# Reading ranks and list sums on ScalarE ahead of the turning back, in an attention and MoE kernel on one core

## The chip, the core and the metric

The kernel runs on one core of a Trainium2 chip. TensorE (PE), VectorE (DVE), ScalarE (ACT) and GpSimd (POOL) run their own instruction streams in program order and meet at semaphores. SyncE (SP) issues most of the DMAs. The metric is device time of one launch in microseconds; the runs of the kernel before took 1053.6, 1046.92 and 1043.89 us, so the median is 1046.92 us. The profiled execution took 1044.68 us and its span from the first to the last instruction is 1042.8 us.

## The reference

Attention with rotated queries and keys over 8 batches of 8 heads, 576 positions and 64 dimensions; then a mixture of experts over the 4608 tokens, where each token goes to the one expert with the largest logit.

```python
q_rot, k_rot = rotate(q), rotate(k)
scores = scale * q_rot @ k_rot.transpose(0, 1, 3, 2)
attn = exp(scores - max); attn /= sum + 1e-09
x = (attn @ v).transpose(0, 2, 1, 3).reshape(B * S, H * D)      # 4608 x 512
logits = x @ w_gate;  e_idx = argmax(logits, axis=1)
gate_w = softmax(logits)[e_idx];  eom = sigmoid(x @ w_output_gate)
for e in range(8):                                              # 512 -> 1024 -> 512
    out[mask_e] = gate_w * eom[:, e] * (relu(x[mask_e] @ w1[e]) @ w2[e])
```

All values are float32. The kernel splits each float32 factor of the scores and of the expert products into a high and a low part and adds three products.

## The kernel before, in words

**Two stages.** The first 540 us or so are the attention, the rest the experts. The attention goes over 32 pairs of heads, four pairs to a batch. A pair has nine steps, one for each unit of 128 rows of scores (the fifth unit holds the last 64 rows of both heads). A unit's scores are six matmuls into a PSUM tile `sc` (`score`, L493), of which there are two. DVE takes their maximum (`peak`, L498), ACT the exponential (`exp`, L507), DVE turns the result by 32x32 blocks (`turn`, L513), and PE multiplies it with the values (`values`, L535). Units go two by two, except the fifth, which goes alone; the program order of one group is: scores, maxima and exponentials of its units, and then, unit by unit, the work that has been put at that step.

**The accumulator of a pair.** The products with the values of a pair go to one PSUM tile `acc` of four banks, of which there is one. Two pairs after its scores, at the second step of a pair, five matmuls turn it back to rows by token and multiply it with the gates (`back`, L553), from a copy in SBUF that ACT made (`evict`, L542 to L544). DVE then divides by the sums (`divide`, four instructions from L560) into `xb`, the rows of the batch. The next pair's products with the values wait until that is done, since they write the same tile. In the traces here, the starts of L560 mark the pace of the attention: one per pair.

**Sorting tokens to experts.** While the next batch's attention runs, the tokens of the batch before are placed (`place`). Its pieces `s0` to `s21` are put at steps counted from PLACE after the batch's last pair; the table `fs` holds (step, place within the step, piece). Three pieces matter here. At step 17 `s14` multiplies the one-hot choices into unused columns of bank 2 of `acc` (the tile that is turned back in that same step): the ranks of the tokens within their expert. `s14b` has DVE add them to the offsets `base` (L690) and to the counts `cnt` (L691). Five times `ones` (L714, DVE) and `places` (L721, POOL) make 0/1 rows from the ranks; `s20` multiplies them into bank 1 of a later pair's `acc` (L729), and `s21` has DVE add the result to `lists` (L732). Both DVE additions stand behind `back` and ahead of `divide` in program order.

**POOL** rotates and splits the keys and queries of coming pairs (L437, L441, L419) and does the small sums of `place`. **SP** loads keys and queries (`raw`, L425), values (`v`, L432) and later the weights, and stores `xb` to the table `xd` in three pieces (`store`, L668, L670). Batch 6 is an exception (`ahead`): its last steps fall behind the end of the attention, and POOL fetches the first tokens of the experts (L1025) beside its first ones.

Of the kernel before, what the change touches and what calls it, by code (L numbers as in the profile page):

```python
# [15 lines left out]
ALU = mybir.AluOpType  # L16
# [6 lines left out]
E, FF = 8, 1024  # L23
P = 128
# [3 lines left out]
NCH = 5  # L28
# [29 lines left out]
PIECES = ((0, 4), (4, 8), (8, 13), (13, 18))  # L58
PLACE, PM = 20, 3
LISTED = 44  # L60
ROWS, PLACES = (28, 30, 32, 37, 39), (25, 29, 31, 34, 38)

TURN = 1

# [178 lines left out]
class Attention:  # L243


    def __init__(self, tc, nb, pools, cc, ident, ii, first, trib, oneb, cnt, zero, qk, v, xd, row, lists):
# [34 lines left out]
        for n, pr in enumerate(self.pairs):  # L281
            g, b = 9 * n, n // NP
            fs = {"kh": lambda pr=pr: pr.keyhi("A"), "kl": lambda pr=pr: pr.keylo("P"),
                  "qh": lambda pr=pr: pr.queryhi("A"), "ql": lambda pr=pr: pr.querylo("P"), "lasts": pr.lasts, "den0": pr.den0, "den1": pr.den1, "den2": pr.den2, "evict": pr.evict, "back": pr.back,
                  "newxb": lambda pr=pr, b=b: newxb(b) if pr.hp == 0 else None}
            fs["divide"] = lambda pr=pr, b=b: pr.divide(xbs[b])
            for t in range(2):
                fs[f"mult{t}"] = lambda pr=pr, t=t: pr.mult("P", t)
                fs[f"add{t}"] = lambda pr=pr, t=t: pr.add("P", t)
                fs[f"load{t}"] = lambda pr=pr, t=t: pr.load(t)  # L290
                fs[f"loadv{t}"] = lambda pr=pr, t=t: pr.loadv(t)
            for k, (b0, b1) in enumerate(PIECES):
                fs[f"av{k}"] = lambda pr=pr, b0=b0, b1=b1: [pr.values(j) for j in range(b0, b1)]
            early = dict(PREP.get(n, ()))
            for name, o, k in EVENTS:
                if n > 1 or name not in ("load1", "load0", "mult1", "add1", "kh", "kl", "mult0", "add0", "qh", "ql")[:10 if n == 0 else 2]:
                    at(g + early.get(name, o), k, fs[name])
            if n % NP == NP - 1:
                fs = place(tc, (px, px2, small), self.pairs, b, NT, cc, trib, oneb, cnt, xbs, xd, row, lists)
                if b == nb - 1:  # L300
                    self.last = fs
                else:
                    for k, p, f in fs:
                        at(g + PLACE + k, p, f)
# [57 lines left out]
class Pair:  # L362
# [183 lines left out]
    def back(self):  # L546

        parts = []
        for c in range(NCH):
            o = PO if c < 4 else PO + BW  # L550
            parts.append((self.acc[:, c % 4, o:o + BW], self.ac[:, c, :, :].rearrange("p a x -> p (a x)")))
        for out, x in parts:
            self.nc.tensor.matmul(out, x, self.ii[:, self.hp, :], start=True, stop=True, skip_group_check=True)  # L553
# [25 lines left out]
def place(tc, pools, pairs, b, NT, cc, trib, oneb, cnt, xbs, xd, row, lists):  # L579

    nc = tc.nc
    p1, p2, small = pools

    last, ahead = b == NT // S - 1, b == NT // S - 2
    V = nc.vector if last else nc.gpsimd
    tt = V.tensor_tensor
    b3 = lambda t: t.unsqueeze(2).broadcast_to((P, NCH, E))
    T = {}

    def new(n, sh, dt=F32, **k):  # L590
        T[n] = p2.tile(sh, dt, tag=n, name=f"{n}{b}", **k)
        return T[n]
# [56 lines left out]
    def add(c):  # L649
        tt(out=T["ohs"][:, c + 1, :], in0=T["ohs"][:, c, :], in1=T["ohb"][:, c, :], op=ALU.add)  # L650

    def s10():
        V.tensor_scalar(T["eg"], T["eg"], 1.0, None, op0=ALU.add)

    def s11():
        tt(out=T["eg"], in0=T["eg"], in1=T["sm"], op=ALU.mult)

    def s12():
        nc.vector.reciprocal(T["eg"], T["eg"])

    def s13():

        V.tensor_copy(xbs[b][:, :, DM], T["eg"])

    def store(i):
        r, n = b * S + i * 2 * P, 2 if i < 2 else 1
        if i < 2:
            nc.sync.dma_start(out=xd[r:r + 2 * P, :].rearrange("(c p) d -> p c d", p=P), in_=xbs[b][:, 2 * i:2 * i + 2, 0:XW])  # L668
        else:
            nc.sync.dma_start(out=xd[r:r + QR, :], in_=xbs[b][0:QR, 4, 0:XW])  # L670
# [10 lines left out]
    def s14():  # L681
# [3 lines left out]
        nc.tensor.matmul(flat(rk), oneb, flat(T["ohs"]), start=True, stop=False, skip_group_check=True)  # L685
        nc.tensor.matmul(flat(rk[:, 0:NCH, :]), trib, flat(T["ohb"]), start=False, stop=True, skip_group_check=True)

    def s14b():
        tt, rk = nc.vector.tensor_tensor, T["rk"]
        tt(out=new("pr", CE), in0=rk[:, 0:NCH, :], in1=T["base"].unsqueeze(1).broadcast_to((P, NCH, E)), op=ALU.add)  # L690
        tt(out=cnt, in0=rk[:, NCH, :], in1=cnt, op=ALU.add)  # L691

# [3 lines left out]
    def s16():  # L696
        nc.vector.tensor_reduce(new("po", [P, NCH]), T["pr"], axis=AX.X, op=ALU.add)
# [11 lines left out]
    def ones(c):  # L709

        if c == 0:
            new("ro", [P, NCH, lists.shape[1]], F32R, bufs=1)
            new("no", [P, NCH])
        nc.vector.tensor_scalar(T["ro"][:, c, :], row, T["hr"][:, c:c + 1], 0.0, op0=ALU.is_equal, op1=ALU.add,  # L714
                                accum_out=T["no"][:, c:c + 1])

    def places(c):

        if c == 0:
            new("pl", [P, NCH, P], F32R, bufs=1)  # L720
        V.tensor_scalar(T["pl"][:, c, :], row[:, 0:P], T["lo"][:, c:c + 1], T["tok"][:, c:c + 1], op0=ALU.is_equal,  # L721
                                op1=ALU.mult)
# [6 lines left out]
            nc.tensor.matmul(T["ls"], T["pl"][0:m, c, :], T["ro"][0:m, c, :], start=(c == 0), stop=(c == 4), skip_group_check=True)  # L729

    def s21():
        nc.vector.tensor_tensor(out=lists, in0=T["ls"], in1=lists, op=ALU.add)  # L732

    def both(f, c):
        return lambda: (f(), add(c))
# [1 line left out]
    no = lambda: None  # L737
    stores = lambda: [store(i) for i in range(3)]
    if last:
        run = lambda *fs: lambda: [f() for f in fs]  # L740
        return [s0, run(s1, s2), s3, run(s4, s5), run(s6, s7), run(s8, add0), both(s9, 1), lambda: [add(c) for c in (2, 3, 4)],
                run(s10, s11, s12), run(s13, base), no, no, no, no, s14, no, s14b, run(s15, s16, s17)] + [
                lambda c=c: (ones(c), places(c)) for c in range(NCH)] + [stores, no, s20, no, s21, no]

    def adds(*cs):
        return lambda: [add(c) for c in cs]

    fs = [(0, 2, s0), (2, 2, s1), (3, 2, s2), (5, 2, s3), (8, 2, s4), (9, 2, s5), (10, 2, s6), (11, 2, s7), (12, 2, add0),
          (12, 2, adds(1, 2)), (13, 2, adds(3, 4)), (15, 2, s8), (15, 2, base), (17, 1, s14), (17, 2, s14b), (18, 2, s9),
          (19, 2, lambda: (s10(), s11())), (20, 2, s15), (22, 2, lambda: (s16(), s12())), (23, 2, s17)]  # L750
    listed = LISTED - 9 if ahead else LISTED
    fs += [(listed, 1, s20), (listed, 2, s21)]
    fs += [(26 + c if ahead else ROWS[c], 3, lambda c=c: ones(c)) for c in range(NCH)]
    fs += [(26 + c if ahead else PLACES[c], 3, lambda c=c: places(c)) for c in range(NCH)]

    if b == NT // S - 2:
        fs += [(37, 2, lambda: (s13(), stores()))]
    else:
        fs += [(25, 2, s13), (31, 2, lambda: store(0)), (33, 2, lambda: store(1)), (34, 2, lambda: store(2)), (37, 2, no)]
    return fs  # L760


# [493 lines left out]
```

## Time and profile before

| | |
|---|---|
| median of 3 runs | 1046.92 us (1043.89 to 1053.6) |
| the profiled execution | 1044.68 us, span 1042.8 us, mean granted TensorE clock 0.990 |
| busy share of the span | PE 93%, DVE 78%, ACT 59%, POOL 57% |
| chain that ended last | PE 60%, DVE 13%, POOL 10%, issue 8%, ACT 6% |

The page lists the busy time of every engine, the chain of waits that ended last, and the groups of instructions. A timeline row has the start, the time from the first start to the last end, the engine and line, the instruction with its output and inputs, how many stand in the row, and in brackets the engine's idle time before it with what ended it. "issue" is idle time that ends without a wait which the profile shows.

### The profile page before, as it was taken

To read this page: it belongs to the slowest core of one execution; us is meant where nothing else is said; L and a number is where in the kernel's file an instruction comes from. 1 tells how busy PE (TensorE), PEld (TensorE's weight loads), DVE (VectorE), ACT (ScalarE), POOL (GpSimd) and SP (SyncE) were. 2 spreads that over 40 slices of the span, in tenths; PEclk is the share of its full clock that TensorE was granted. 3 is DMA by queue.
4 is the path that set the end of the run, shared out by engine and by line. 5 is a ranking of instruction groups with operands and counts; after the bars stand their busy time and mean duration, and the time that the engine had idled before them with its cause. 6 is when DMAs were issued, how large, how long until landed. Compare 5 with 4: busy or idle time off the path is not lost.

```text
span 1042.8 us, 34822 instructions
## 1 busy us (share of the span) xinstructions
PE 969.2 (93%) x14461; PEld 844.4 (81%) x14461; DVE 818.0 (78%) x1371; ACT 616.8 (59%) x1283; POOL 599.6 (57%) x613
## 2 busy tenths in 40 slices
PE   4999999989999999999799999999999999999995
PEld 4778777767878777777678899998889988899984
DVE  6889989979988898998768777667776867857772
ACT  4656656656655566665445455557766765857762
POOL 4777898887988879889640122206343443443621
PEclk9999999999999999999999999999999999999998
DMA  6665664666745657465548966767886977977860
GB/s 218 164 173 130 179 195 128 177 163 167 198 125 163 185 159 205 118 179 147 160 140 299 300 211 201 230 201 254 312 299 216 356 243 268 325 283 257 299 240 29
DMA packets 58209, 216.32 MB, mean 207 GB/s; under 512 B 9351, under 2 KB 9660, under 8 KB 53952
## 3 DMA queue, kind: packets, MB, share of 16 engines
q1 hardware_dynamic: 50304, 194.03, 59.9%
q0 software_dynamic: 6464, 18.92, 5.0%
q8 instruction: 115, 1.88, 0.8%
q10 hardware_dynamic: 1280, 1.11, 0.3%
q14 instruction: 46, 0.38, 0.1%
HBM read 196.04 MB, written 20.09 MB: 207 GB/s over the span
## 4 chain that ended last, share of the span: by engine, by line
PE 60%; DVE 13%; POOL 10%; issue 8%; ACT 6%; DMA 1%; ACTq 0%; POOLq 0%; DVEq 0%
PE py L1132 17%; PE ph L1090 14%; PE sc L493 11%; PE acc L535 9%; DVE m L498 5%; POOL raw L437 4%; PE ph L1082 4%; ACT pm L507 4%; DVE pt L513 2%; DVE wl L1049 2%; PE acc L553 2%; POOL raw L441 1%; PE mtp L1055 1%; POOL q L419 1%; ACT wh L1047 1%
## 5 line engine op out<-in xcount | busy, mean ns | idle before, releaser
L507 ACT ACTIVATE pm<-sc,m 128x576 f32<-128x576 f32 x288 | 211.1, 737 | 208.7 <-DVE m L498 207.5
L1049 DVE TENSOR_TENSOR wl<-wr,wh 128x1024 fp32r<-128x1024 f32 x184 | 251.9, 1381 | 45.2 <-ACT wh L1047 42.8
L498 DVE TENSOR_REDUCE m<-sc 128x1 f32<-128x576 f32 x288 | 205.7, 748 | 58.6 <-PE sc L493 57.6
L535 PE MATMUL acc<-pt,v 32*64 32x128 f32 (+1 forms) x9216 | 201.3, 298 | 31.2 <-issue 18.5
L493 PE MATMUL sc<-kh,q 64*128 64x288 f32 x1024 | 205.2, 325 | 20.7 <-ACT q L411 9.7
L1132 PE MATMUL py<-wh,ht 128*128 128x512 f32 x640 | 215.4, 401 | 0.0
L1047 ACT CAST wh<-wr 128x1024 fp32r<-128x1024 f32 x208 | 212.6, 1050 | 0.0
L513 DVE STREAM_TRANSPOSE pt<-pm 128x576 f32<-128x576 f32 x288 | 208.9, 753 | 0.0
L535 PEld LDWEIGHTS acc<-pt,v 32*64 32x64 f32 x9216 | 160.9, 133 | 57.1 <-issue 38.9
L493 PEld LDWEIGHTS sc<-kh,q 64*128 64x128 f32 x1024 | 153.1, 191 | 53.6 <-ACT pm L507 23.1
L437 POOL TENSOR_TENSOR raw<-raw,rt 128x1152 f32<-128x1152 f32 x62 | 163.9, 2643 | 0.3
L1090 PE MATMUL ph<-xt,wh 128*128 128x256 f32 x896 | 161.1, 282 | 0.5 <-DVE xt L1071 0.5
L1132 PEld LDWEIGHTS py<-wh,ht 128*128 128x128 f32 x640 | 120.3, 188 | 25.7
L1090 PEld LDWEIGHTS ph<-xt,wh 128*128 128x128 f32 x896 | 138.3, 188 | 2.4 <-DVE xt L1071 1.2
L493 PE MATMUL sc<-kl,q 64*128 64x288 f32 x512 | 129.7, 308 | 0.0
L1090 PE MATMUL ph<-xt,wl 128*128 128x256 f32 x448 | 126.1, 281 | 0.0
L1132 PE MATMUL py<-wl,ht 128*128 128x512 f32 x320 | 125.9, 393 | 0.0
L1049 POOL TENSOR_TENSOR wl<-wr,wh 128x1024 fp32r<-128x1024 f32 x24 | 58.3, 2431 | 90.4 <-ACT wh L1047 84.4
L441 POOL TENSOR_TENSOR raw<-raw 128x576 f32<-128x576 f32 x62 | 87.6, 1413 | 1.9
L1106 ACT ACTIVATE ht<-ph 128x512 fp32r<-128x512 f32 x56 | 33.4, 597 | 90.3 <-PE ph L1090 90.3
L493 PEld LDWEIGHTS sc<-kl,q 64*128 64x128 f32 x512 | 86.3, 192 | 0.2 <-DVE kl L419 0.2
L1090 PEld LDWEIGHTS ph<-xt,wl 128*128 128x128 f32 x448 | 84.3, 188 | 0.1
(247 smaller groups left out, 1317.4 us busy)
## 6 DMA issues: line engine op xcount, KB each, us to landing
wr<-in_w SPq DMA_DIRECT2D x208, 512.0 KB
raw<-in_qk SPq DMA_DIRECT2D x64, 576.0 KB
v<-in_v SPq DMA_DIRECT2D x128, 288.0 KB
xd<-xb SPq DMA_DIRECT2D x16, 513.0 KB
xd<-xb SPq DMA_DIRECT2D x8, 128.2 KB
rt<-in_rope ACTq DMA_DIRECT2D x1, 576.0 KB
xg<-xd,2idx POOLq DMA_INDIRECT x18, 6.7
out<-y,2idx POOLq DMA_INDIRECT x18, 3.9
```

The lines of the kernel that those rows point to most:

```text
L437: self.eng(eng).tensor_tensor(out=rv, in0=rv, in1=self.rt[:, 2 * t:2 * t + 2, x], op=ALU.mult)
L441: self.eng(eng).tensor_tensor(out=r[:, 2 * t, x], in0=r[:, 2 * t, x], in1=r[:, 2 * t + 1, x], op=ALU.add)
L493: self.nc.tensor.matmul(self.ps[i][:, a, :HS], st, mov[r, x], start=(n == 0), stop=(n == 2))
L498: nc.vector.tensor_reduce(self.m[i], ps[:, :, :HS], axis=AX.XY, op=ALU.max, negate=True)
L507: nc.scalar.activation(pe.rearrange("p (a b) -> p a b", a=2), self.ps[i][:, :, :HS], AF.Exp, bias=self.m[i], scale=1.0, accum_out=self.z[: ...
L513: self.nc.vector.transpose(out=self.pt[:, st[0] + 5 * st[1] if st else 4, :], in_=self.pc.pop(i))
L535: nc.tensor.matmul(self.acc[h * D:h * D + D, a, o:o + 32 * n], self.v[r, h, j, :], self.pt[r, u:u + n, 32 * j:32 * j + 32], start=(j == 0) ...
L1047: self.nc.scalar.copy(wh, r)
L1049: eng.tensor_tensor(out=wl, in0=r, in1=wh.bitcast(F32), op=ALU.subtract)
L1082: nc.tensor.matmul(ph[:, 0, :], st[:, dc, 0:P], mv[:, dc, :], start=(n == 0), stop=(n == 11))
L1090: nc.tensor.matmul(ph[:, f, :], st[:, dc, fs], mv[:, dc, :], start=(n == 0), stop=(n == 11))
L1132: self.nc.tensor.matmul(py[h], st[:, f, hs], mv, start=(f == 0 and n == 0), stop=(f == 7 and n == 2))
```

## The change

Ranks: ACT copies the ranks from PSUM to a new tile `rc` as soon as `s14` has made them (`s14c`, put ahead of `back` in the same step), and POOL makes the two additions of `s14b` from that copy one step later. Lists: ACT copies the sums to `lc`, put ahead of `back`, and POOL adds them to `lists` one step later (`s22`). `back` writes the banks in the order 0, 3, 0, 1, 2. `base` moves from step 15 to step 6. `ones` moves from steps 28, 30, 32, 37, 39 to 29, 29, 38, 38, 42 (for batch 6 from 26 to 30 to 29, 29, 29, 33, 33). The second and third store move from steps 33 and 34 to 40 and 42.

```diff
-ROWS, PLACES = (28, 30, 32, 37, 39), (25, 29, 31, 34, 38)
+ROWS, AHEAD, PLACES = (29, 29, 38, 38, 42), (29, 29, 29, 33, 33), (25, 29, 31, 34, 38)
...
     def back(self):
         parts = []
-        for c in range(NCH):
+        for c in (0, 3, 4, 1, 2):
...
+    def s14c():
+        rc = new("rc", [P, NCH + 1, E])
+        nc.scalar.copy(rc, T["rk"])
+        T["rk"] = rc
+
     def s14b():
-        tt, rk = nc.vector.tensor_tensor, T["rk"]
+        rk = T["rk"]
         tt(out=new("pr", CE), in0=rk[:, 0:NCH, :], in1=T["base"].unsqueeze(1).broadcast_to((P, NCH, E)), op=ALU.add)
         tt(out=cnt, in0=rk[:, NCH, :], in1=cnt, op=ALU.add)
...
     def s21():
-        nc.vector.tensor_tensor(out=lists, in0=T["ls"], in1=lists, op=ALU.add)
+        if last:
+            nc.vector.tensor_tensor(out=lists, in0=T["ls"], in1=lists, op=ALU.add)
+            return
+        nc.scalar.copy(new("lc", [P, lists.shape[1]], bufs=1), T["ls"])
+
+    def s22():
+        nc.gpsimd.tensor_tensor(out=lists, in0=T["lc"], in1=lists, op=ALU.add)
...
-          (12, 2, adds(1, 2)), (13, 2, adds(3, 4)), (15, 2, s8), (15, 2, base), (17, 1, s14), (17, 2, s14b), (18, 2, s9),
+          (12, 2, adds(1, 2)), (13, 2, adds(3, 4)), (6, 2, base), (15, 2, s8), (17, 1, s14), (17, 1, s14c), (18, 2, s14b), (18, 2, s9),
...
-    fs += [(listed, 1, s20), (listed, 2, s21)]
-    fs += [(26 + c if ahead else ROWS[c], 3, lambda c=c: ones(c)) for c in range(NCH)]
+    fs += [(listed, 1, s20), (listed, 1, s21), (listed + 1, 2, s22)]
+    fs += [((AHEAD if ahead else ROWS)[c], 3, lambda c=c: ones(c)) for c in range(NCH)]
...
-        fs += [(25, 2, s13), (31, 2, lambda: store(0)), (33, 2, lambda: store(1)), (34, 2, lambda: store(2)), (37, 2, no)]
+        fs += [(25, 2, s13), (31, 2, lambda: store(0)), (40, 2, lambda: store(1)), (42, 2, lambda: store(2)), (37, 2, no)]
```

TensorE's stream at the ranks of the first batch (step 17), before; L685 and L686 are `s14`, L553 is `back`, L493 the scores of the next two units, and a name in brackets is the engine whose semaphore the instruction waits for:

```order
L493 MATMUL sc_1_2076<-kh_1826,q_1915 128x288
L685 LDWEIGHTS oneb [waits Activation_49]
L685 MATMUL acc_1834<-ohs_1948,oneb 128x48 [waits Pool_49]
L686 LDWEIGHTS trib
L686 MATMUL acc_1834<-ohb_1918,trib 128x40
L553 MATMUL acc_1834<-ii,ac_117 128x160 x5
L493 MATMUL sc_2_2119<-kh_1826,q_1915 128x288 [waits Activation_49]
```

The same place in the changed program:

```order
L493 MATMUL sc_1_2076<-kh_1828,q_1917 128x288
L685 LDWEIGHTS oneb [waits Activation_49]
L685 MATMUL acc_1836<-ohs_1950,oneb 128x48 [waits Pool_49]
L686 LDWEIGHTS trib
L686 MATMUL acc_1836<-ohb_1920,trib 128x40
L553 MATMUL acc_1836<-ii,ac_117 128x160 [waits Activation_49]
L553 MATMUL acc_1836<-ii,ac_117 128x160 x4
L493 MATMUL sc_2_2118<-kh_1828,q_1917 128x288 [waits PE_49]
```

The first matmul of `back` has got a wait for ACT, and the scores behind it have lost theirs.

ScalarE's stream at that place in the changed program; L507 are the exponentials of the two units of this step, L690 is the copy of `s14c`, L465 belongs to the next pair:

```order
L543 COPY ac_117<-acc_1836 64x64
L544 COPY ac_117<-acc_1836 64x64
L507 ACTIVATE pm_0_2093,z_115<-sc_0_2075,m_0_2089 128x576 [waits DVE_49,Activation_49,Pool_49]
L507 ACTIVATE pm_1_2095,z_115<-sc_1_2076,m_1_2091 128x576 [waits DVE_49,Activation_49]
L690 COPY rc_2102<-acc_1836 128x48 [waits PE_49]
L465 CAST bd_114<-q_1917 64x2x64 [waits Pool_49]
```

The copy stands behind both exponentials; before, L465 followed them directly. The copy of the list sums stands at the same place, three pairs further on.

VectorE's stream in the pair with the first `ones`, before (L714):

```order
L498 TENSOR_REDUCE m_4_2502<-sc_4_2495 128x1 [waits DVE_49,PE_49]
L513 STREAM_TRANSPOSE pt_2386<-pm_3_2449 128x576 [waits Activation_49]
L498 TENSOR_REDUCE m_5_2557<-sc_5_2543 128x1 [waits DVE_49,PE_49]
L498 TENSOR_REDUCE m_6_2559<-sc_6_2544 128x1 [waits DVE_49,PE_49]
L513 STREAM_TRANSPOSE pt_2386<-pm_4_2504 128x576 [waits Activation_49]
L714 TENSOR_SCALAR ro_2492,no_2493<-row,hr_2330 128x288
L513 STREAM_TRANSPOSE pt_2386<-pm_5_2561 128x576 [waits Activation_49]
```

and in the changed program (L719):

```order
L498 TENSOR_REDUCE m_4_2501<-sc_4_2494 128x1 [waits DVE_49,PE_49]
L513 STREAM_TRANSPOSE pt_2388<-pm_3_2451 128x576 [waits Activation_49]
L719 TENSOR_SCALAR ro_2541,no_2542<-row,hr_2332 128x288 x2
L498 TENSOR_REDUCE m_5_2560<-sc_5_2546 128x1 [waits DVE_49,PE_49]
L498 TENSOR_REDUCE m_6_2562<-sc_6_2547 128x1 [waits DVE_49,PE_49]
L513 STREAM_TRANSPOSE pt_2388<-pm_4_2503 128x576 [waits Activation_49]
```

Two of them now stand together ahead of the maximum of the sixth unit, and none stands between two transposes.

## Rows read from the trace of the kernel before

**Rows 1.** Busy time by stretch: length, busy us of each engine, PE clock, DMA.

```profile
110.00:460.00 350.00, 320.78 (x7669) 269.64 (x7668) 308.66 (x598) 208.73 (x570) 297.44 (x343) 0.99 0.59 163
600.00:900.00 300.00, 299.13 (x1954) 270.09 (x1953) 215.45 (x293) 186.85 (x264) 106.15 (x69) 1.00 0.75 255
```

**Rows 2.** Timeline of DVE: starts of the division, L560, one per pair.

```profile
109.87 0.68 DVE L560 TENSOR_TENSOR xb<-acc,rz 128x512 f32<-128x512 f32 x1
125.75 0.68 DVE L560 TENSOR_TENSOR xb<-acc,rz 128x512 f32<-128x512 f32 x1
140.77 0.65 DVE L560 TENSOR_TENSOR xb<-acc,rz 128x512 f32<-128x512 f32 x1
157.99 0.65 DVE L560 TENSOR_TENSOR xb<-acc,rz 128x512 f32<-128x512 f32 x1
174.31 0.68 DVE L560 TENSOR_TENSOR xb<-acc,rz 128x512 f32<-128x512 f32 x1
...
271.89 0.65 DVE L560 TENSOR_TENSOR xb<-acc,rz 128x512 f32<-128x512 f32 x1
287.63 0.65 DVE L560 TENSOR_TENSOR xb<-acc,rz 128x512 f32<-128x512 f32 x1
```

**Rows 3.** Timeline of DVE at the ranks of the first batch.

```profile
122.19 1.42 DVE L498 TENSOR_REDUCE m<-sc 128x1 f32<-128x576 f32 x2 [0.19 <-PE sc L493]
...
125.56 0.20 DVE L690 TENSOR_TENSOR pr<-acc,base 128x40 f32<-128x40 f32 x1 [0.61 <-POOL base L673]
```

**Rows 4.** Timeline of PE at the ranks of the first batch.

```profile
122.64 0.18 PE L686 MATMUL acc<-ohb,trib 128*128 128x40 bf16 x1
122.67 1.60 PE L553 MATMUL acc<-ii,ac 128*128 128x160 f32 x10
...
127.02 1.35 PE L535 MATMUL acc<-pt,v 32*64 32x160 f32 x64 [1.28 <-issue]
```

**Rows 5.** Timeline of ACT at the ranks of the first batch.

```profile
122.15 0.21 ACT L544 COPY ac<-acc 64x64 f32<-64x64 f32 x1
...
123.80 0.73 ACT L507 ACTIVATE pm<-sc,m 128x576 f32<-128x576 f32 x1
...
124.51 0.60 ACT L465 CAST bd<-q 64x128 fp32r<-64x128 f32 x2
```

**Rows 6.** Timelines of DVE, PE and ACT at the list of the first batch.

```profile
170.61 1.42 DVE L498 TENSOR_REDUCE m<-sc 128x1 f32<-128x576 f32 x2 [0.27 <-PE sc L493]
...
173.74 0.46 DVE L732 TENSOR_TENSOR lists<-acc,lists 128x288 f32<-128x288 f32 x1 [0.36 <-PE acc L553]
...
172.07 1.62 PE L553 MATMUL acc<-ii,ac 128*128 128x160 f32 x10
...
170.01 0.58 ACT L542 COPY ac<-acc 128x512 f32<-128x512 f32 x1
...
172.91 0.59 ACT L465 CAST bd<-q 64x128 fp32r<-64x128 f32 x2
```

**Rows 7.** Timeline of DVE: a wait for scores, and one of `ones`.

```profile
116.08 1.42 DVE L498 TENSOR_REDUCE m<-sc 128x1 f32<-128x576 f32 x2 [0.86 <-PE sc L493]
...
149.53 0.47 DVE L714 TENSOR_SCALAR_CACHE_REDUCE ro<-row,hr 128x288 fp32r<-128x288 bf16 x1
```

**Rows 8.** Timeline of PE: a stop without a wait, and a gap followed by slower matmuls.

```profile
216.03 0.41 PE L493 MATMUL sc<-kh,q 64*128 64x288 f32 x2 [2.05 <-issue]
...
321.84 1.97 PE L535 MATMUL acc<-pt,v 32*64 32x160 f32 x64 [1.27 <-issue]
```

**Rows 9.** Busy time by stretch, with the PE clock, behind two gaps.

```profile
217.00:220.00 3.00, 3.00 (x84) 2.68 (x82) 2.60 (x6) 1.55 (x4) 3.00 (x2) 0.50 0.70 207
516.00:524.00 8.00, 4.06 (x75) 3.46 (x76) 4.13 (x11) 1.65 (x5) 3.04 (x7) 0.57 1.00 362
```

**Rows 10.** Timeline of DVE at the ranks of batch 6.

```profile
511.26 1.42 DVE L498 TENSOR_REDUCE m<-sc 128x1 f32<-128x576 f32 x2 [0.19 <-PE sc L493]
...
518.49 0.20 DVE L690 TENSOR_TENSOR pr<-acc,base 128x40 f32<-128x40 f32 x1 [4.46 <-POOL base L673]
```

**Rows 11.** Timeline of PE at the list of batch 6.

```profile
548.12 1.62 PE L553 MATMUL acc<-ii,ac 128*128 128x160 f32 x10
```

## The prediction, made before the run

> **What bounds the kernel now.** I read the stretches first. In the attention no engine is full: over 350 us PE is busy for 320.8 us and DVE for 308.7 [rows 1], so the pace is set by who waits for whom within a pair. In the expert stage PE is busy for 299.1 of 300 us [rows 1]; what the attention loses or gains before it moves the end by as much. Next I read the starts of the division, one per pair [rows 2]. From 125.75 to 140.77 is a pair with almost no sorting work: 15.02 us. The pair with the ranks before it took 15.88, the one with three `ones` after it 17.22, the one with two `ones` and the list 16.32. In a quieter batch the pair with three `ones` took 15.74 (271.89 to 287.63). What the change can touch is this excess over 15.0 us.
>
> **The ranks, batches 0 to 5.** Before, the maxima of the two units start at 122.19 and the division at 125.75, behind DVE's wait of 0.61 us for POOL's `base` and the two additions [rows 2, 3]. `back` was not in the way: PE started it at 122.67, right behind `s14`, and took 1.60 us [rows 4]. The change takes wait and additions off DVE. But the order of the changed program shows a wait for ACT on the first matmul of `back`, none on the other four, and none for ACT any more on the scores that follow, which had waited for the exponentials before. So the first one waits for something behind both exponentials, and what stands there is the copy to `rc`. ACT reaches it at 124.51 [rows 5]. 48 columns cost at most the 0.21 us of a copy with 64 [rows 5]; with 0.1 us for the signal `back` starts at 124.82, ends 1.60 later at 126.42, and the division starts at about 126.5: 0.75 us later than before, six times: **+4.5**. DVE's saved work doesn't count, since DVE waits anyway. POOL's two extra sums lie in its waits for ACT.
>
> Which banks must wait is also a matter of rule. The Trainium skill, PSUM — Partial Sum Buffer, section "PSUM bank collisions raise a hardware error", says that two engines must not be in the same bank and quadrant at once and that different banks run clean; by that `back` could begin in banks 0 and 3 while ACT reads bank 2. No row of before shows the two together. In the sum I follow the wait in the program; the other case is the first rival.
>
> **The lists, batches 0 to 5.** Before, DVE waited 0.36 us for `back`, added for 0.46 and divided at 174.31 [rows 2, 6]. Now `back` waits for the copy to `lc`, which ACT reaches at 172.91 instead of the L465 there [rows 6]. 288 columns lie between 0.21 us for 64 [rows 5] and 0.58 for 512 [rows 6]; on the line between them 0.40. `back` then starts at 173.41 instead of 172.07, takes 1.62 [rows 6], and the division starts at 175.08: 0.77 later, six times: **+4.6** (+3.5 to +5.7 with the copy at either end). POOL's addition of 288 columns lies in slack.
>
> **`ones`, batches 0 to 5.** Three in one pair cost 0.72 us where nothing else went wrong (15.74 less 15.02) [rows 2]. Now two stand where DVE waits 0.86 us for scores in every pair [rows 7]; at 0.47 each at most [rows 7] they overrun it by 0.1. Six times 0.6: −3.7. In the next pair two `ones` had cost 16.32 less 15.02 less the list's share. That share is 0.93: the division started 3.70 after the maxima [rows 2, 6], and with nothing between it would start 2.77 after them, two rows of 1.42 less their overlap. So 0.37 for the two; now 0.1 for the two in the wait and 0.20 for the one ahead of a wait of 0.27 [rows 6]. Together **−4.1**.
>
> **Batch 6.** At its ranks DVE waited 4.46 us for `base`, which POOL made behind four fetches [rows 10]. `base` now comes long before them. With the spacing worked out above (maxima to division 126.5 less 122.19, or 4.3 us) the division starts at 515.6 instead of 518.7: −3.1. The PE clock stood at 0.57 on average around it [rows 9]; if the shorter gap keeps it up, between 0 and 2.0 us of the 4.06 us of matmuls there come back. I take 0.6, near the lower end, because most of them lie beside DVE's work. At its list PE has no other work and is the bound: `back` starts 0.6 later than 548.12 [rows 11], +0.6. Together **−3.1**.
>
> **The stores.** The same bytes leave one pair later. In the pair in which all three were stored, PE stops for up to 2.05 us in the middle of matmuls with no wait that the trace shows [rows 8], and such a pair took 17.22 where the quietest took 15.74 [rows 2]: 1.48 us. If all such stops go, five batches give −7.4; if they only move with the stores, 0, or even +7.4 if they come twice. I take **−1.5**, near zero, because the transfers remain.
>
> **The clock.** `back` now leaves PE idle from 122.82, the end of `s14` [rows 4], to 124.82: 2.0 us, in place of the gap of 1.28 us that stood at 127.02 [rows 4]. A gap of 2.05 us was followed by 3.00 us at half the clock, 1.2 for 2.4 GHz [rows 8, 9]. A gap of 1.28 us was not: the 64 matmuls behind it took 1.35 us [rows 4], and the same 64 took 1.97 behind another gap of 1.27 [rows 8]. So at 2.0 us it may fall or not. Half the clock for 3.00 us of matmuls costs up to 1.5 us; for three of the six at 1.2, less the one that falls already, I take **+2.4**, between 0 and 9.
>
> The Trainium skill, TensorE: Matmul & The Clock Gate, section "The HAM clock gate", has it that idleness halves the clock and that the moment isn't tied to the kernel's start; the two gaps of 1.27 and 1.28 us that ended differently agree.
>
> **Sum.** +4.5 +4.6 −4.1 −3.1 −1.5 +2.4 = +2.8 us on the profiled 1044.68 us: 1047.5. That execution stands 2.2 us below the median of the three runs, 1046.92. I predict **1047 us**: no change that can be told.
>
> **Rivals.** *`back` waits only at the bank that is read.* Then three of its five products run at once and two remain behind the copy. At the ranks the last product (a fifth of 1.60) would end at 125.14, and the division start 0.55 earlier than before; at the lists the last two end at 174.05, 0.2 earlier. The two terms become −3.3 and −1.2 and the clock term goes: 1047 less 9.1 less 2.4 less 4.5, about 1031. Against it stands the wait on the first matmul of `back` in the order. 0.08.
>
> *The stops of PE vanish with the spread stores.* Then −7.4 instead of −1.5: about 1041. For it: they stand in the pair of the stores; against it: the load of `v` and `raw` goes on. 0.17.
>
> *Every new gap halves the clock.* At the ranks seven gaps of 2.0 us, at the lists six of 1.34 (172.07 to 173.41). Seven falls at 1.5, less the 2.4 counted, give 1055; with the six at the lists 1064. It decides between 1.28 us, which was mostly harmless, and 2.05, which was not. For it the row at 217 [rows 9], against it the clock of 0.99 over the attention [rows 1], which holds six gaps of nearly 1.3. 0.17, half of it beyond 1057.
>
> The forecast itself gets 0.58.
>
> **Range and chances.** About 1% is what a measurement of this kernel can tell from no change; that is 1036.5 to 1057.4. Faster than that: the first rival and a part of the second with runs on the low side, 0.13. Slower: half of the third and a part of the forecast with its bounds at the upper end, 0.14. Between: 0.73. The low end of 1036 holds the vanished stops with a kind clock; the first rival lies outside it. The high end of 1058 holds the clock falling at all ranks.
>
> **What would show it.** Right: in the changed profile `back` starts behind the copy to `rc`, about 2.2 us after the first of `s14`, with a wait for ACT; the division starts 4.2 to 4.4 us after the maxima at the ranks and about 4.5 at the lists; the wait of 0.86 us for scores is gone where two `ones` stand; the 4.46 us wait at batch 6 is gone. Wrong: `back` starting right behind `s14`, or pairs with ranks at 15.3 us. The forecast fails most easily by the clock and by the stops, which no order of instructions shows.

## The result, and the profile after

The changed kernel took **1059.51 us**, median of ten runs (1054.49 to 1067.08), beside 1049.01 us for the kernel before, now also of ten runs (1043.89 to 1054.17): ratio **1.0103, 95% interval 1.0076 to 1.013**. The forecast was 1047 us and no change. A later repeat gave 1.013 (1.0077 to 1.0183). The profiled execution took 1063.05 us, its span 1061.2, where before it was 1044.68 and 1042.8. These two single executions differ by 18.4 us, the medians by 10.5: what is read below from the two traces is larger than the median loss.

First the stretches, the columns as in [rows 1].

```profile
110.00:460.00 350.00, 314.29 (x7321) 264.78 (x7318) 293.71 (x559) 201.12 (x554) 291.27 (x344) 0.96 0.57 157
600.00:900.00 300.00, 298.56 (x1931) 268.36 (x1930) 215.83 (x308) 180.63 (x252) 98.48 (x65) 1.00 0.75 257
```

In the attention fewer instructions of every engine but POOL fit into the same 350 us, and the mean PE clock is 0.96 instead of 0.99. The middle of the expert stage is as full as before. The divisions, one per pair, on DVE's timeline:

```profile
110.16 0.68 DVE L560 TENSOR_TENSOR xb<-acc,rz 128x512 f32<-128x512 f32 x1
126.89 0.69 DVE L560 TENSOR_TENSOR xb<-acc,rz 128x512 f32<-128x512 f32 x1 [1.66 <-PE acc L553]
142.69 0.65 DVE L560 TENSOR_TENSOR xb<-acc,rz 128x512 f32<-128x512 f32 x1
158.17 0.65 DVE L560 TENSOR_TENSOR xb<-acc,rz 128x512 f32<-128x512 f32 x1
179.23 0.69 DVE L560 TENSOR_TENSOR xb<-acc,rz 128x512 f32<-128x512 f32 x1 [2.21 <-issue]
...
562.20 0.69 DVE L560 TENSOR_TENSOR xb<-acc,rz 128x512 f32<-128x512 f32 x1 [1.70 <-PE acc L553]
```

Against [rows 2] the pair with the ranks went from 15.88 to 16.73 us, the next from 15.02 to 15.80, the pair with the first `ones` from 17.22 to 15.48, the one with the list from 16.32 to 21.06. The last division stood at 550.16 before:

```profile
550.16 0.68 DVE L560 TENSOR_TENSOR xb<-acc,rz 128x512 f32<-128x512 f32 x1
```

From there to the end of the span it was 492.6 us before and 499.0 now. So 12.0 us were lost in the attention and **6.4 us behind it**, where the forecast had seen nothing. Not all of the 6.4 is net: the pair that ends with the last division took 13.84 us, where it had taken 15.72.

PE at the ranks of the first three batches and of batch 4, and at the first list with a stop ahead of it, to be held against [rows 4, 6]:

```profile
122.92 0.18 PE L686 MATMUL acc<-ohb,trib 128*128 128x40 bf16 x1
125.03 1.75 PE L553 MATMUL acc<-ii,ac 128*128 128x160 f32 x10 [1.94 <-ACT rc L690]
...
165.90 0.28 PE L493 MATMUL sc<-kh,q 64*128 64x288 f32 x1 [1.87 <-issue]
...
176.82 2.31 PE L553 MATMUL acc<-ii,ac 128*128 128x160 f32 x10 [1.28 <-ACT lc L740]
...
194.76 3.03 PE L553 MATMUL acc<-ii,ac 128*128 128x160 f32 x10 [1.94 <-ACT rc L690]
...
263.70 3.04 PE L553 MATMUL acc<-ii,ac 128*128 128x160 f32 x10 [1.94 <-ACT rc L690]
...
397.58 1.63 PE L553 MATMUL acc<-ii,ac 128*128 128x160 f32 x10 [1.95 <-ACT rc L690]
```

The first product of `back` waits for the copy, 1.94 us at the ranks and 1.28 at the list, as forecast. The last number to read is how long `back` itself takes: 1.63 us where the clock held, 3.03 where it fell. The stretches behind the gaps say the same; the third column from the end is the clock:

```profile
177.00:179.50 2.50, 2.50 (x14) 2.17 (x15) 0.29 (x2) 0.26 (x1) 1.41 (x4) 0.62 0.68 140
194.50:196.50 2.00, 1.74 (x6) 1.74 (x7) 0.46 (x1) 0.69 (x5) 1.92 (x2) 0.54 1.03 230
397.50:400.00 2.50, 2.42 (x21) 2.25 (x22) 0.96 (x3) 0.51 (x3) 2.34 (x3) 1.00 1.04 221
573.00:581.00 8.00, 7.04 (x19) 5.36 (x20) 7.52 (x9) 6.03 (x9) 0.00 (x0) 0.57 1.03 412
```

Behind four of the six waits at ranks of batches 0 to 5 and one of the six at lists the clock went to 1.2 GHz, and behind three of PE's stops without a wait. Before, there were three such falls in the attention. In the pair of 21.06 us several things meet: PE stops for 1.87 us at 165.90 without a wait, and the clock falls behind that stop and again behind the wait for the list.

The end of the attention, on POOL, in batch 6:

```profile
546.23 3.92 POOL L726 TENSOR_SCALAR pl<-row,lo,tok 128x128 fp32r<-128x128 bf16 x5
560.51 0.79 POOL L743 TENSOR_TENSOR lists<-lc,lists 128x288 f32<-128x288 f32 x1 [10.36 <-ACT lc L740]
561.25 0.19 POOL L663 COPY xb<-eg 128x5 f32<-128x5 f32 x1
```

and on SP's queue and PE:

```profile
561.46 0.90 SPq L668 DMA_DIRECT2D xd<-xb  x2
562.45 0.85 SPq L670 DMA_DIRECT2D xd<-xb  x1
563.50 25.51 SPq L1049 DMA_DIRECT2D wr<-in_w  x16
...
573.29 0.59 PE L1143 MATMUL py<-wh,ht 128*128 128x512 f32 x1 [2.46 <-ACT wh L1058]
```

This is the wait that nobody had asked after. The list's addition, now POOL's, waits 10.36 us for the list. The copy of the tokens' gate weights (`eg`) into `xb` stands behind it, the stores of batch 6 behind that on SP's queue, and the loads of the expert weights `wr` behind the stores: they begin at 563.50. Before, on POOL and SP:

```profile
536.17 0.20 POOL L663 COPY xb<-eg 128x5 f32<-128x5 f32 x1
...
538.44 1.18 SPq L1038 DMA_DIRECT2D wr<-in_w  x1
```

In the changed kernel PE then waits 2.46 us for its first converted weights, and its clock falls (573 to 581, mean 0.57).

### The profile page after: what moved, and what is told of

Same layout as the page of the kernel before. It is cut to its first block, busy times and chain, and to the rows that moved or that the text cites. A ratio compares the mean times of both kernels' runs of the same rounds, so it can differ in the third digit from the quotient of the medians.

```text
span 1061.2 us, 34844 instructions
## 1 busy us (share of the span) xinstructions
PE 977.9 (92%) x14461; PEld 852.8 (80%) x14461; DVE 813.9 (77%) x1350; ACT 619.8 (58%) x1297; POOL 608.4 (57%) x634
## 4 chain that ended last, share of the span: by engine, by line
PE 68%; DVE 12%; issue 8%; ACT 6%; POOL 2%; DMA 2%; POOLq 0%; ACTq 0%; SPq 0%; DVEq 0%
PE py L1143 19%; PE sc L493 15%; PE ph L1101 14%; PE acc L535 12%; DVE m L498 5%; ACT pm L507 5%; PE ph L1093 4%; PE acc L553 2%; DVE pt L513 2%; PE mtp L1066 2%; DVE wl L1060 1%; DMA wr<-in_w 1%; DVE xb L560 1%; DVE xb L562 1%; ACT wh L1058 1%
## 5 line engine op out<-in xcount | busy, mean ns | idle before, releaser
L507 ACT ACTIVATE pm<-sc,m 128x576 f32<-128x576 f32 x288 | 211.1, 737 | 220.5 <-DVE m L498 217.8
L493 PE MATMUL sc<-kh,q 64*128 64x288 f32 x1024 | 205.6, 333 | 20.8 <-ACT q L411 9.4
L1058 ACT CAST wh<-wr 128x1024 fp32r<-128x1024 f32 x208 | 213.0, 1050 | 6.3 <-DMA wr<-in_w 6.2
L535 PE MATMUL acc<-pt,v 32*64 32x160 f32 (+1 forms) x9216 | 200.9, 299 | 16.7 <-PE sc L493 8.5
L493 PEld LDWEIGHTS sc<-kh,q 64*128 64x128 f32 x1024 | 154.7, 197 | 51.5 <-issue 21.9
L493 PE MATMUL sc<-kl,q 64*128 64x288 f32 x512 | 130.3, 317 | 0.0
L493 PEld LDWEIGHTS sc<-kl,q 64*128 64x128 f32 x512 | 88.7, 198 | 2.2 <-issue 1.9
```

The lines of the kernel that those rows point to most:

```text
L493: self.nc.tensor.matmul(self.ps[i][:, a, :HS], st, mov[r, x], start=(n == 0), stop=(n == 2))
L507: nc.scalar.activation(pe.rearrange("p (a b) -> p a b", a=2), self.ps[i][:, :, :HS], AF.Exp, bias=self.m[i], scale=1.0, accum_out=self.z[: ...
L535: nc.tensor.matmul(self.acc[h * D:h * D + D, a, o:o + 32 * n], self.v[r, h, j, :], self.pt[r, u:u + n, 32 * j:32 * j + 32], start=(j == 0) ...
L1058: self.nc.scalar.copy(wh, r)
```

## The experiments

Each ratio is to the kernel before, with its 95% interval; for e1 to e12 the runs of the kernel before are from the same chip. Rows compared with each other can be from different chips, and then only by their ratios. "To the end" is the time from the last division to the end of the span in the kernel's profiled execution.

| kernel | ratio | median us | last division | to the end |
|---|---|---|---|---|
| before | 1 | 1049.01 | 550.16 | 492.6 |
| changed | 1.0103 (1.0076 to 1.013) | 1059.51 | 562.20 | 499.0 |
| e1 copies behind `back` | 0.9908 (0.9875 to 0.9941) | 1043.49 | 541.97 | 502.9 |
| e2 no copies | 0.9881 (0.9837 to 0.9924) | 1038.77 | 540.71 | 492.6 |
| e3 copies only | 1.017 (1.0127 to 1.0214) | 1068.57 | 564.34 | 500.5 |
| e7 filler on PE | 1.0057 (1.0022 to 1.0093) | 1055.85 | 553.61 | 500.5 |
| e8 list of batch 6 on DVE | 1.0061 (1.0026 to 1.0095) | 1061.98 | 566.89 | 493.4 |
| e9 e1 and e8 | 0.9843 (0.9813 to 0.9873) | 1036.84 | 544.84 | 493.1 |
| e4 stores only | 0.9936 (0.9909 to 0.9962) | 1045.00 | 546.04 | 493.0 |
| e5 `ones` only | 0.9992 (0.9969 to 1.0015) | 1050.61 | 553.33 | 492.9 |
| e6 `base` only | 0.9915 (0.9886 to 0.9945) | 1045.81 | 550.61 | 493.0 |
| e10 changed, again | 1.013 (1.0077 to 1.0183) | 1067.11 | 559.47 | 499.6 |
| e11 e7 and e8 | 1.000 (0.9965 to 1.0035) | 1053.20 | | |
| e12 e9, stores in five | 0.987 (0.9829 to 0.9912) | 1041.47 | 547.91 | 492.8 |

The kernel before had medians of 1052.75 beside e1 to e3 and e7, 1052.48 beside e4, e5, e8, e9, and 1053.99 beside the last four.

**e1, the copies behind `back`.**

```
-(17, 1, s14c)           +(17, 2, s14c)
-(listed, 1, s21)        +(listed, 2, s21)
```

> The changed kernel with both copies asked for one phase later, behind back in the program: ACT copies at the same place in its own queue, but back no longer waits for it (the copy waits for back). All else of the change stays. Theory C (the waits ahead of back, and the PE clock that falls behind them): 13 gaps of 1.3 to 2.0 us on PE go, so 9 us of later divisions and 4 to 7 us of half clock come back: 1044 to 1048 us, ratio to the kernel before 0.994 to 0.999, and no fall of the clock within 2 us behind the ranks. Theory W (the waits alone, the clock costs nothing): 1050 us. Theory S (PE's stops, which the later stores made longer, carry the loss): 1055 to 1060.

Faster than the changed kernel by some 2%, more than theory C had asked for. Theory S falls, and so does the sum of theory W, 1050 us: nothing but the order of copy and `back` differs. Whether the clock has a price of its own is left to e7 and e11. The pairs with ranks take 15.02 to 15.04 us in five batches and 15.56 in the sixth, hardly more than a pair without sorting work: the copy takes DVE's additions away and nobody waits for it. At the lists the division does wait for the copy, 0.57 us in the quietest pair (15.85 us). The quietest pairs of the changed kernel took 16.66 us with ranks and 16.80 with a list; over six batches the difference makes some 15.5 of the 20.5 us between the two ratios. But to the end it is 502.9 us, and PE waits 6.44 us for the first converted weights. That led to e8 and e9. The first two rows are on DVE's timeline of e1, the divisions around the ranks of batch 0, the third is a division behind a list; the last is on PE's timeline:

```profile
113.11 0.68 DVE L560 TENSOR_TENSOR xb<-acc,rz 128x512 f32<-128x512 f32 x1
128.14 0.65 DVE L560 TENSOR_TENSOR xb<-acc,rz 128x512 f32<-128x512 f32 x1
...
305.56 0.69 DVE L560 TENSOR_TENSOR xb<-acc,rz 128x512 f32<-128x512 f32 x1 [0.57 <-ACT lc L740]
...
556.71 0.79 PE L1143 MATMUL py<-wh,ht 128*128 128x512 f32 x1 [6.44 <-ACT wh L1058]
```

**e2, no copies.** DVE adds from PSUM as before; the rest of the change stays.

```
-(17, 1, s14c), (18, 2, s14b)                  +(17, 2, s14b)
-(listed, 1, s21), (listed + 1, 2, s22)        +(listed, 2, s21)
```

> The changed kernel without its copies: DVE adds from PSUM behind back as in the kernel before; the order of the banks, the moved ones, the earlier base and the later stores stay. Theory C: 1043 to 1048, the gains of ones and batch 6 of 7 us against the kernel before less what the stops cost. Theory W: 1050. Theory S: 1055 to 1060. Beside the kernel with the copies behind back it tells what the copies save on DVE: DVE's saved work of 0.46 us per list is worth at most 6 x 0.4 = 2.4 us, and at the ranks nothing, if DVE waits anyway.

1.2% faster than before, better than expected, and 492.6 us to the end. So the copies, with the late weights that come with them, carry the whole loss of the change and more; without them it gains.

**e3, the copies alone.** The kernel before with `s14c`, the new `s21` and `s22`.

> The kernel before with the copies ahead of back and GpSimd's addition alone; ones, base, stores and banks as before. Theory C: +9.1 us for the waits and +4 to +7 for the clock: 1062 to 1066 us, ratio 1.012 to 1.016. Theory W: +9.1: 1058, ratio 1.009. Theory S: the copies are worth their waits at most, and less where DVE's saved work counts: 1053 to 1057, ratio below 1.008.

+1.7%, or 17.9 us of 1053: at the upper end of theory C and a little beyond, out of reach of S. The late weights are in it (500.5 to the end), and with some 0.6% for them theory W would come to 1.015 and lie inside the interval: e3 alone doesn't part W from C. Its quietest pairs took 16.64 us with ranks (15.88 before) and 17.08 with a list (16.32 before).

**e7, filler.** Ahead of `s14` five products with `back`'s operands, ahead of `s20` three, into columns that `back` overwrites.

```
+def fill(n):
+    p = pairs[...]
+    for _ in range(n):
+        nc.tensor.matmul(p.acc[:, 3, PO:PO + BW], p.ac[:, 3, ...], p.ii[:, p.hp, :], start=True, stop=True, ...)
...
+(17, 1, lambda: fill(5)), (17, 1, s14), ...
```

> The changed kernel with five more products of 128x160 (those of back, whose result is overwritten) ahead of the ranks' matmuls and three ahead of the lists' in batches 0 to 5: PE works in the gap, and back still waits for the copy, whose place in ACT's queue the extra work (1.6 us and 1.0 us) doesn't move. Theory C: the clock no longer falls behind the ranks and lists, the divisions stay as late as in the changed kernel: 4 to 8 us faster than it, 1051 to 1055. Theory W: no change, 1059 to 1060. Theory S: no change or slower by the products that don't fit, 1059 to 1062.

The wait of `back` shrinks because PE works until shortly before the copy is done. PE's timeline of e7 at the ranks of batch 0, and at one of batch 1:

```profile
122.33 1.62 PE L684 MATMUL acc<-ii,ac 128*128 128x160 f32 x10
...
123.83 0.18 PE L692 MATMUL acc<-ohb,trib 128*128 128x40 bf16 x1
124.49 1.63 PE L553 MATMUL acc<-ii,ac 128*128 128x160 f32 x10 [0.49 <-ACT rc L696]
...
195.04 1.63 PE L553 MATMUL acc<-ii,ac 128*128 128x160 f32 x10 [0.49 <-ACT rc L696]
```

In all twelve rows of `back` behind a copy in batches 0 to 5, `back` takes 1.62 or 1.63 us, and the pairs with ranks still take 16.63 to 16.68: the wait costs what it did, the clock's fall behind it is gone. The mean PE clock from 110 to 460 us is 0.99, as before the change, against 0.96 in the changed kernel. On DVE's timeline of e7, the divisions around the ranks of batch 0:

```profile
109.60 0.68 DVE L560 TENSOR_TENSOR xb<-acc,rz 128x512 f32<-128x512 f32 x1
126.23 0.69 DVE L560 TENSOR_TENSOR xb<-acc,rz 128x512 f32<-128x512 f32 x1 [1.54 <-PE acc L553]
```

Against the changed kernel that is 0.46%, 4.8 us (0.2 to 9.5); the two intervals meet, so e11 repeats it. One rival stays: the filler also moves other instructions to the places where PE stops without a wait (last section). In e7's profile these stops are 6 with 8.1 us, in the changed kernel's 7 with 11.1, so a part of the 4.8 us may be theirs.

**e8, the list of batch 6 on DVE**, all other copies as in the change.

```
 def s21():
-    if last:
+    if last or ahead:
         nc.vector.tensor_tensor(out=lists, in0=T["ls"], in1=lists, op=ALU.add)
```

> The changed kernel with the list of batch 6 alone added by DVE from PSUM, behind back, as before; all other copies stay ahead of back. Theory Q: in the changed kernel GpSimd's addition of that list waits 10.36 us for its copy, the copy of the weights into xb stands behind it on GpSimd (561.25), the stores behind that on SP's queue (561.46) and the experts' weight loads behind the stores (563.50), so PE waits 2.46 us for its first expert weights and the clock falls. Without it the time from the last division to the end goes back from 499.0 to the 492.6 us of the kernel before: 1052 to 1054 us, ratio to before 1.003 to 1.005, and no wait of PE for wh above 1 us. Rival: the weights come late because DMA is busy then: no change, 1058 to 1060.

To the end it is 493.4 us, and PE has no wait for `wh` of even 0.5 us there: the chain over POOL and SP is confirmed. By the two ratios it is worth 0.42%, 4.4 us, with an interval that reaches zero. The ratio went from 1.0103 to 1.0061, a little short of theory Q's 1.003 to 1.005, and by this pair alone the intervals overlap; in the profiled execution the clock fell behind four ranks and all six lists, so its attention was long.

**e9, both taken out.** The edits of e1 and e8 together.

> The copies behind back, and the list of batch 6 added by DVE: both suspected costs of the change taken out. Theory C with Q: the 1043.5 us of the kernel with the copies behind back, less the 6 to 10 us that its expert stage is longer than that of the kernel without copies (502.9 against 492.6 us from the last division to the end): 1034 to 1038 us, ratio 0.982 to 0.988, level with the kernel without copies (1038.8) or up to 4 us better. Rival (the weights are late for another reason): 1043.

The lowest ratio of the study: 1.6% faster than before, 2.6% than the changed one. Against e1 it gains 0.65%, 6.8 us (2 to 11.5), by the list of batch 6 alone. On POOL and SP in batch 6 of e9:

```profile
531.05 0.20 POOL L663 COPY xb<-eg 128x5 f32<-128x5 f32 x1
...
531.27 0.90 SPq L668 DMA_DIRECT2D xd<-xb  x2
532.26 0.84 SPq L670 DMA_DIRECT2D xd<-xb  x1
533.31 34.83 SPq L1051 DMA_DIRECT2D wr<-in_w  x17
```

The copy comes at 531.05, before the last division (544.84) instead of nearly with it, and the weights follow at 533.31. Between e9 and e2 the measurement doesn't decide.

**e10 and e11, the change again and the two suspects out together.** e11 has the filler of e7 and the edit of e8.

> The changed kernel itself once more, beside the next two on the same chip: ratio to the kernel before 1.008 to 1.013, 1057 to 1063 us.

> The changed kernel with the list of batch 6 added by DVE and with the filler products ahead of the ranks' and lists' matmuls: the late weight loads and the idle PE behind ranks and lists are both taken out, while back still waits for its copies. Theory C with Q: 4 to 5 us below the kernel with the list of batch 6 by DVE alone (1.0061), ratio 1.000 to 1.003, 1050 to 1054 us, and no fall of the clock behind a rank or list gap. Theory W (the clock costs nothing): 1.005 to 1.007, as without the filler.

1.013 against 1.000, side by side: 1.3%, some 14 us of 1054, with intervals that don't meet, although `back` waits for its copies in batches 0 to 5 of both. That is the price of the idle PE's clock and of the late weights together, with whatever the filler does to PE's stops; the waits themselves are not in it. From e8 to e11 the filler gives 0.61% (0.1 to 1.1), from the change to e7 0.46%: theory W, by which the filler changes nothing, falls. The granted clock of all runs, not only the profiled ones, says the same: its median is 0.982 in the changed kernel and 0.988 in e7, 0.980 in e8 and 0.989 in e11. In the 26 runs of the kernel before beside e8, 0.01 of mean clock goes with some 9 us (a straight line through their times, 0.977 to 0.989), so an estimate from these numbers is 5 us for the first pair and 8 for the second. (The profiled execution of e11 is not read here.)

**e4, e5 and e6, the other parts, each alone in the kernel before.**

```
e4: -(33, 2, store(1)), (34, 2, store(2))        +(40, 2, store(1)), (42, 2, store(2))
e5: -ROWS = (28, 30, 32, 37, 39), ahead 26 + c   +ROWS, AHEAD = (29, 29, 38, 38, 42), (29, 29, 29, 33, 33)
e6: -(15, 2, s8), (15, 2, base)                  +(6, 2, base), (15, 2, s8)
```

> The kernel before with the second and third store of each batch at the later places, nothing else. Theory S (the later stores make PE's stops longer): slower by 5 us or more, 1054 to 1058, ratio 1.005 to 1.01. Rival (PE stops where its next 16 KiB of instructions comes late behind any DMA traffic, so that stops move and don't go): within 3 us of before, ratio 0.997 to 1.003. The prediction's term: -1.5 us; its rival: -7.4.

> The kernel before with the ones at their new places alone. The prediction's term: -4.1 us, ratio 0.996; rival: in the changed kernel two ones in DVE's wait still cost 0.45 us a pair over 15.02, so six pairs with ones give 6 x (0.72 - 0.47) = 1.5 and what the next pair saves, 2 us, ratio 0.998 to 1.0; and if the ones moved into the pair with the loads lengthen PE's stops, 1.0 to 1.003.

> The kernel before with base summed at step 6 instead of 15, nothing else. The prediction's own step: -3.1 at batch 6 by the wait of 4.46 us, and at the other ranks DVE's wait of 0.61 us for POOL's base goes, worth up to 6 x 0.5 = 3: ratio 0.994 to 0.997. What the kernel without copies (0.9881) leaves when the stores (0.9936) and the ones (0.9992) are taken from it is 0.9953. Rival: the wait at the ranks is followed by another, batch 6 alone counts: 0.997 to 1.0.

The stores gain 0.64%, 6.7 us (4.0 to 9.6): both theories missed it, and theory S falls for good. PE's stops of over 0.5 us between 40 and 540 us at the fixed places of the last section are 4 with 5.1 us in e4's profile, 8 with 9.0 before. In other kernels with the same later stores they are 6 to 9 with 6.7 to 12.8 us, so it isn't shown that fewer stops are the cause. The median granted clock is 0.989 in e4 and 0.985 in the kernel before beside it, which by the 9 us for 0.01 above is some 4 us of the 6.7; why it is higher stays open. The `ones` give 0.8 us, nothing that can be told. `base` gains 0.85%, 8.9 us (5.8 to 12.0), more than expected: the ranks of batch 6 went from 19.73 to 15.51 us and those of the other batches from 15.88 to between 15.16 and 15.44, some 8 us together. The new order of the banks in `back` was never run alone.

**e12, smaller stores.** e9 with each batch's stores cut into five.

```
-(31, store(0)), (40, store(1)), (42, store(2))
+((28, 31, 36, 40, 42)[c], 2, lambda c=c: store1(c)) for c in range(NCH)
```

> The copies behind back and the list of batch 6 on DVE (0.9843, 1036.8 us), with each batch's three stores cut into five of at most 128 rows at steps 28, 31, 36, 40 and 42. Theory F (PE stops at the end of a 16 KiB page of its instructions when the fetch of the next page stands behind data on the DMA queues): smaller bursts delay fetches less, the 10 stops of 12.1 us between 40 and 540 us shrink by 2 to 6 us, ratio 0.979 to 0.983. Rival: the loads of v and raw alone make the fetch late, as large as they are: unchanged, 0.983 to 0.987.

Not faster, and the stops grew from 9 with 12.2 us to 14 with 18.1 in the one profile of each. That PE's stops would shrink with the size of a store is not borne out.

## Why the prediction was wrong

**Waits ahead of `back`: right.** At the ranks the forecast was a start 2.2 us behind `s14`, a division 4.3 us behind the maxima, and +0.75 a pair. It came out at 2.15, 4.42 (122.47 to 126.89), and at +0.75 to +0.80 where the clock held (16.63 to 16.68 in e7, against 15.88 to 15.90). At the lists the quietest pairs went from 16.32 to 16.80, the moved `ones` included. In e3, where nothing else was moved, the quietest pairs went up by 0.76 at both places, 9.1 us for the twelve. The copy to `rc` took 0.20 us, that to `lc` 0.40, as estimated; `back` started 0.04 and 0.05 us behind their ends, where 0.1 us had been taken for the signal without a row. The rival in which `back` waits only for the bank that is read fell: its products in other banks waited too.

**"POOL's addition of 288 columns lies in slack": wrong, and the step that failed without any bound.** In batches 0 to 5 it is so. In batch 6 the addition has 10.36 us to wait and the weights' column, the stores and the expert weights behind it. Priced at nothing, it cost 4.4 us by e8 against the changed kernel and 6.8 by e9 against e1; behind the last division it is 6.4 in the changed kernel's profile. The five profiles with that addition on POOL that are read here show 499.0 to 502.9 us to the end, the eight with it on DVE 492.6 to 493.4. Some of that comes back ahead of the last division: the last pair takes 13.2 to 13.8 us in the five and 15.0 to 17.3 in the eight. No run shows why. What the prediction did for the ranks, naming what is queued behind the waiting instruction, it did not do here.

**The clock: mis-sized.** Taken at +2.4 us, with three of six gaps at the ranks, measured at 4.8 (e7) and 6.4 (e11 against e8), each with an interval of some 5 us to either side and with PE's moved stops in it. The gaps at the lists were counted as harmless at 1.28 us because one such gap before had been: that was too thin. Of the same wait of 1.25 to 1.28 us at the lists one in six was followed by a fall in the changed kernel, six in six in e8, and two in five in e10, which is the changed kernel again. The third rival named the mechanism, but without the late weights its 1055 would have been too low as well.

**The stores: mis-sized.** Taken at −1.5, measured at −6.7 alone (e4), near the end of −7.4 that stood as the second rival. In the changed kernel's own profile the stops did not get fewer in time: 7 with 11.1 us where before there were 8 with 9.0.

**`ones`: mis-sized.** Taken at −4.1, measured at −0.8 (−3.3 to +1.6). The two in the wait fit as drawn: on DVE's timeline of the changed kernel the wait of [rows 7] is gone,

```profile
148.04 0.47 DVE L719 TENSOR_SCALAR_CACHE_REDUCE ro<-row,hr 128x288 fp32r<-128x288 bf16 x1
...
148.44 0.51 DVE L719 TENSOR_SCALAR_CACHE_REDUCE ro<-row,hr 128x288 fp32r<-128x288 bf16 x1
...
148.99 1.42 DVE L498 TENSOR_REDUCE m<-sc 128x1 f32<-128x576 f32 x2
```

and the pair took 15.48. But e5's pairs with `ones` range from 16.9 to 18.9 us, because PE's stops fall there, and the 0.6 us each don't show beside them.

**Batch 6 and `base`: the wait as forecast, the number partly by luck, and a gain overlooked.** The wait of 4.46 us is gone, and the last three pairs took 46.51 us instead of 51.22: −4.7 where −3.1 was forecast. Of this −2.1 lies in the pair with the ranks and −1.9 in the last pair, for which +0.6 was forecast and which is short in every kernel with late weights. Alone, `base` gains at every rank; in the change the copy ahead of `back` takes this away again, since DVE there waits for `back` anyway. So the parts don't add up: copies, stores, `ones` and `base` alone give +1.7, −0.64, −0.08 and −0.85%, together +0.13, where the change has +1.03.

**The sum with measured terms:** waits +9.1, `ones` −0.8, batch 6 −4.7, stores −6.7, clock +5.6 (between its two measurements), late weights +6.4 (behind the last division, in the same profile as the −4.7): +8.9 us. The whole was measured at 8.0 to 13.6 us (1.0076 to 1.013 of 1049). The parts overlap, since stores and `ones` were measured without the copies, and the intervals of the clock alone leave room for several us either way.

**The base of the sum.** The forecast put its +2.8 us on the one profiled execution, 1044.68 us, while ten runs of the kernel before have a median of 1049.01. Of the 12 us between the 1047.5 of the sum and the measured 1059.51, 4.3 are this base and 7.7 the terms.

## What to carry to other kernels

In this program a copy out of a PSUM tile that was put ahead of the tile's next writer made that writer wait, 1.94 us at the ranks; put behind it, the same copy was free at the ranks and cost the division 0.57 us at a list, and 2% of the kernel lay between the two orders. When work moves to an engine with slack, look at each place where it will wait there, the last batch above all, and follow what is queued behind it through every queue to the loads of the next stage. A new gap on PE costs more than its length where the clock falls behind it. A filler can tell the two prices apart, as long as one also looks at what else it moves.

## What the runs showed of the hardware

**PE's stops without a wait stand at fixed places of its instruction stream.** Counting all of PE's instructions in the trace (weight loads, matmuls and the few of its sequencer), the stop at 223.04 in the changed kernel comes at PE's instruction 8386, and that at 216.03 of before [rows 8] at the same one. Others stand at 1218, 5570, 6081, 8897, 11202, 14018, 17090, 19650: all multiples of 256 apart, give or take one, and the stops of the other kernels read here, up to 540 us, stand on the same grid. (The gaps ahead of the 64 value products behind ranks and lists, "issue" too in the trace, stand off this grid.) In e7, where eight products per batch were added, the numbers stayed on this grid and the code at them changed. The stop of the changed kernel, PE's timeline:

```profile
219.65 1.64 PE L535 MATMUL acc<-pt,v 32*64 32x160 f32 x80
223.04 0.41 PE L493 MATMUL sc<-kh,q 64*128 64x288 f32 x2 [1.76 <-issue]
```

The DMA queues of the changed kernel from 212.0 to 220.2 us (packets, MB, share of 16 engines):

```profile
q1 hardware_dynamic: 416, 1.39, 74.9%
q14 instruction: 1, 0.01, 0.2%
```

and from 220.2 to 223.0:

```profile
q1 hardware_dynamic: 80, 0.33, 45.8%
q8 instruction: 1, 0.02, 2.8%
```

Queue q8 carries 16 KiB of instructions a packet, 115 in the whole run. For over 8 us of data traffic no such packet came; the next started at 220.41, took 1.24 us, and PE went on 1.4 us behind its end. In all profiles of this study PE goes on 1.1 to 1.8 us behind the end of such a packet at every one of these stops. In the changed kernel the packets ahead of the seven stops came 6.8 to 10.2 us behind the one before, the others 5.4 us in the median; but some of the others came as late and no stop followed (8.9 us, the one at 200.99). So the late packet is shown, while that the data ahead of it delays the fetch is only a guess that fits; smaller stores did not cure it in e12, and what sets the delay stays open. The Trainium skill, Runtime: NRT & Kernel Launch, section "Instruction fetch mechanics", has blocks of 16 KiB, 256 instructions, and calls the cost of crossing into the next one "mostly hidden". The grid agrees; the cost doesn't here: 7 stops with 11.1 us in the attention of the changed kernel.

**The same gap doesn't always end alike.** Behind waits of 1.94 us `back` took 1.63 us or up to 3.04, in one and the same execution; behind waits of 0.49 to 0.53 us always 1.62 or 1.63.
